# First query-weight load split over unequal DMA engines, with probability copies and key transposes regrouped on VectorE

## The chip, the cores and the metric

The kernel runs on one core of one Trainium2 chip. The metric is the device time of one execution in microseconds (us); the number given for a kernel is the median of several executions. A profile is one further execution, recorded by the hardware profiler; it gives the time from the first to the last instruction (the span), each engine's instructions, and the packets of the core's 16 DMA engines.

## The reference

One decode step for two rows of `x` (B = 2, one token each, D = 512), everything in float32. The layer-normed row `xn` feeds two branches, and both are added to `x`:

```python
q = (xn @ wq)                               # 32 heads of 128
k, v = the last W = 4096 positions of the caches, 8 kv heads, each shared by 4 q heads
p = softmax(q k^T * 128**-0.5);  o = p v
A = o @ wo                                   # (2, 4096) @ (4096, 512)
h = relu(xn @ W_gate) * (xn @ W_up)          # 1792 wide
B = h @ W_down
out = x + A + B
```

The keys and values that are needed are 2 x 8 x 4096 x 128 floats each, 32 MB and 32 MB (of 4,096 KB tiles: eight and eight); wq and wo are 8 MB each, the three GLU weights 3.5 MB each.

## The kernel before

All large inputs come in as tiles of [128 partitions x up to 32 KB] through one pool of four buffers (`ring`, line 60), and every one of these loads is issued by SyncE (`load`, lines 69 to 72, and lines 438 to 442). SyncE issues in the order of the program and waits, before each load, until the tile that used that buffer four loads earlier has been read for the last time. A load that is issued joins a queue behind the loads before it. The order is wq0, wq1, W_gate, W_up, two key tiles, then key and value tiles in turn, the last two value tiles, W_down, wo0 and wo1; wo1 goes in five pieces of 8, 4, 2, 1 and 1 rows of 2 KB per partition (line 438).

`load_wq` (lines 75 to 77) brings one half of wq: partition p holds two whole rows of wq, 32 KB that lie side by side in memory, so the load is 128 rows of 32 KB.

The work is cut in four groups g (two batches by two halves of the kv heads), each with two key tiles and two value tiles (a = 0, 1). `manual_schedule` means that each engine runs its instructions in the order in which the program writes them.

`keys(g, a, ...)` (line 243) treats a key tile in two halves mh. For each half VectorE turns 32 x 32 blocks of the key tile into `kT` (line 252). One half is 64 positions j of 64 numbers, [128 x 4096], and it is turned by CUT = 4 instructions of 16 positions each, [128 x 1024]. Then eight matmuls (line 259, order m, h, s1) add to the scores in `ss[g]`; a matmul with s1 = 0 reads the first 32 positions of `kT`, one with s1 = 1 the other 32. `kT` has two buffers.

`softmax(g)` (line 268) takes the maximum on VectorE and TensorE and writes the exponentials into `pz` on ScalarE (line 291). `turn(g)` (line 295) turns `pz` into `pT` with one VectorE instruction (line 297) and then moves 16 blocks of [32 x 256] from `pT` to `pts[g]` (line 304), the stationary operand of the value matmuls: the even ones on ScalarE, the odd ones on VectorE. `values(g, a, v)` (line 317) multiplies them by a value tile. In the loop (line 385) the keys and the softmax of group g stand ahead of the values of group g - 1, and `turn(g)` behind them; `join` and `close` (mask, gather, normalise) are put between the halves of the next key tile.

The end: the last value tiles, then `project_wide` and `project` (lines 418 to 428) with W_down, wo0 and wo1 as these land, the last piece of wo1 with four matmuls on line 426, one copy from PSUM (line 453), and two small stores (line 456).

Of the kernel before, what the change touches and what calls it, by code (L numbers as in the profile page):

```python
# [9 lines left out]
F32 = mybir.dt.float32  # L10
# [10 lines left out]
def kernel(  # L21
# [12 lines left out]
    nc = tc.nc  # L34
    P = 128
    B, _, D = x.shape
    _, HKV, SK, DH = k_cache.shape
    HQ = wq.shape[1] // DH
# [15 lines left out]
    J = W // PK  # L54
# [5 lines left out]
    ring = ctx.enter_context(tc.tile_pool(name="ring", bufs=RING))  # L60
# [8 lines left out]
    def load(name, src, shape):  # L69
        t = ring.tile(shape, F32, name=name, tag="ring")  # L70
        nc.sync.dma_start(t, src)
        return t


    def load_wq(m):
        src = wq[m * 2 * P:(m + 1) * 2 * P, :].rearrange("(p k) f -> p k f", p=P)
        return load(f"wq{m}", src, [P, 2, HQ * DH])

    def load_ff(w, name):
        return load(name, w.rearrange("(p k) f -> p k f", p=P), [P, KC, F])  # L80
# [23 lines left out]
    x2 = const.tile([B, D], F32, name="x2")  # L104
    nc.scalar.dma_start(x2, x[:, 0, :])
    wqt = [load_wq(m) for m in range(2)]

    ident = const.tile([P, P], F32, name="ident")
# [68 lines left out]
    for kc in range(KC):  # L177
        m, k = divmod(kc, 2)
# [12 lines left out]
    for kc in range(KC):  # L191
        for r in range(R):
            for c in range(C):
                n = r * C + c
# [6 lines left out]
    for r in range(R):  # L201
# [7 lines left out]
        for m in range(NB):  # L209
            src = qt[32 * m:32 * m + 32, :, :, 0].rearrange("p i (t h) b -> p b t h i", h=2)  # L210
            for x in range(Q):
                d = qz[32 * x:32 * x + 32, r * B:r * B + B, m]
                dst = bass.AP(
                    tensor=d.tensor, offset=d.offset + x * TK,
                    ap=[d.ap[0], d.ap[1], [64 + REP, NP], [32, 2], [1, REP]],
                )
# [21 lines left out]

    ss, pts = {}, {}
    osb = {}  # L240
    CUT = 4

    def keys(g, a, kt_in, steps=((), ())):

        if a == 0:
            ss[g] = ps_s.tile([P, 512], F32, name=f"s{g}", tag="s")
        for mh in range(2):
            kt = ktp.tile([P, J, 2, 32], F32, name=f"kT{g}_{a}_{mh}", tag="kT")
            src = kt_in.rearrange("p (j d) -> p j d", d=DH)[:, :, PK * mh:PK * mh + PK]
            n = J // CUT  # L250
            for c in range(CUT):
                nc.vector.transpose(  # L252
                    kt[:, c * n:(c + 1) * n].rearrange("p j m i -> p j (m i)"), src[:, c * n:(c + 1) * n]
                )
            for m in range(2):
                for h in range(2):
                    for s1 in range(S1):
                        q = 2 * h + s1
                        nc.tensor.matmul(  # L259
                            ss[g][32 * q:32 * q + 32, :], qz[:, g, 2 * mh + m, a, h], kt[:, JS * s1:JS * s1 + JS, m, h::2],  # L260
                            start=(a == 0 and mh == 0 and m == 0), stop=(a == NP - 1 and mh == 1 and m == 1),
                        )
            for step in steps[mh]:
                step()
# [30 lines left out]
    def turn(g):  # L295
        pT = work.tile([P, JS, Q, NP, REP], F32, name=f"pT{g}", tag="pT", bufs=1)
        nc.vector.transpose(pT.rearrange("p j x t k -> p (j x t k)"), pz.rearrange("p j s -> p (j s)"))  # L297
        pts[g] = work.tile([P, NP, S1, JS, 2, REP], F32, name=f"pt{g}", tag="pt")
        n = 0
        for h in range(2):  # L300
            for s1 in range(S1):
                q = 32 * (2 * h + s1)
                for x in range(Q):
                    (nc.vector.tensor_copy if n % 2 else nc.scalar.copy)(  # L304
                        pts[g][32 * x:32 * x + 32, :, s1, :, h], pT[q:q + 32, :, x].rearrange("p j t k -> p t j k")
                    )
                    n += 1

    lps = {}

# [58 lines left out]
    for a in range(NP):  # L369
        keys(0, a, load_kv(k_cache, "k", 0, a))  # L370
    softmax(0)
    turn(0)
    def join(g, a):
        mask(g, a)
# [10 lines left out]
    for g in range(1, NG):  # L385
        for a in range(NP):
            kt_in = load_kv(k_cache, "k", g, a)
            v_in = load_kv(v_cache, "v", g - 1, a)
            keys(g, a, kt_in, steps)
            if a:  # L390
                softmax(g)
            values(g - 1, a, v_in)
            if a:
                turn(g)
            steps = (
                (lambda g=g, a=a: join(g - 1, a),), (lambda g=g: close(g - 1),) if a else (),
            )
# [87 lines left out]
```

## Time and profile before

| | |
|---|---|
| median of three executions | 230.36 us (230.18 to 230.57) |
| the profiled execution, time / span | 230.8 us / 228.4 us |
| granted TensorE clock, mean over the span | 0.821 |
| TensorE matmuls busy | 143.5 us, 63% of the span |
| VectorE busy | 112.4 us, 49%, 176 instructions |
| ScalarE busy | 27.0 us, 12%, 72 instructions |
| read from HBM | 94.90 MB, 416 GB/s over the span |

How to read the profile: times in a timeline or a chain run from the first instruction. A group's row gives line, engine, operation, tiles (out<-in), shape and count, then busy time in all and the mean duration of one in ns, then the engine's idle time just before these instructions and what ended it. The row "DMA" of the page gives, for 40 equal slices of the span, how busy the 16 DMA engines were in tenths (9 is 90% or more); "GB/s" is what they moved. In a table of windows the last two columns are the mean share of the 16 DMA engines and GB/s. "SPq" is SyncE's sequencer, which issues loads. "q1", "q8", "q10" and "q14" are rows of DMA queues: q1 carries what SyncE issues, q10 what ScalarE issues, q8 and q14 carry instructions that an engine's sequencer fetches.

### The profile page before, as it was taken

What the parts mean: (1) busy time and instruction counts of PE and PEld (TensorE: products, weight loads), DVE (VectorE), ACT (ScalarE), POOL (GpSimd) and SP (SyncE); (2) the same over time, 40 slices, a digit from 0 to 9 for tenths busy, and PEclk for the clock granted to TensorE, in tenths of its full rate; (3) what the DMA queues carried; (4) which work ended last, traced back from release to release, by engine and by line L of the source; (5) the groups of instructions that cost most, each with busy time, mean ns of one, the idle gap of its engine ahead of it and who ended that gap; (6) DMA issues with size and microseconds to landing.
All of it is one profiled execution on the core that took longest, in us unless ns stands there. A gap on an engine that the chain in (4) does not pass through costs nothing.

```text
span 228.4 us, 2114 instructions
## 1 busy us (share of the span) xinstructions
PE 143.5 (63%) x864; PEld 40.1 (18%) x864; DVE 112.4 (49%) x176; ACT 27.0 (12%) x72; POOL 3.7 (2%) x11
## 2 busy tenths in 40 slices
PE   0582927806674038957499196859928757868393
PEld 0530211201111001402013011101401201214011
DVE  2300043049894499865992594797069272120000
ACT  2000123000000720003500000700000160000001
POOL 6000000000000000000000000000000000000000
PEclk9999767795999557997759859767995995999589
DMA  7999999999999999999999999999999999999991
GB/s 276 459 413 412 472 402 422 448 453 419 413 455 442 396 448 445 407 430 453 425 410 453 436 407 442 429 430 425 448 430 419 439 430 418 440 419 448 399 387 44
DMA packets 3917, 95.04 MB, mean 416 GB/s; under 512 B 442, under 2 KB 450, under 8 KB 836
## 3 DMA queue, kind: packets, MB, share of 16 engines
q1 hardware_dynamic: 3896, 94.90, 97.0%
q8 instruction: 7, 0.11, 0.2%
q14 instruction: 2, 0.02, 0.0%
q10 hardware_dynamic: 12, 0.01, 0.0%
HBM read 94.90 MB, written 0.00 MB: 416 GB/s over the span
## 4 chain that ended last, share of the span: by engine, by line
DMA 60%; DVE 21%; PE 13%; ACT 2%; issue 1%; SPq 1%; DVEq 0%; ACTq 0%
DMA k<-in_A_k_cache_dram 39%; DVE kT L252 16%; DMA wo<-in_A_wo_dram 11%; DMA wq<-in_A_wq_dram 9%; PE s L259 5%; PE o L324 4%; PE q_ps L195 2%; DVE pt L304 2%; ACT pz L291 1%; DVE pT L297 1%; DVE on L333 1%; PE oa L344 1%; SPq L441 1%; DVE m L271 1%; ACT L291 1%
## 5 line engine op out<-in xcount | busy, mean ns | idle before, releaser
L259 PE MATMUL s<-kT,qz 128*32 128x512 f32 x256 | 61.5, 780 | 43.7 <-DVE kT L252 43.7
L252 DVE STREAM_TRANSPOSE kT<-k 128x1024 f32<-128x1024 f32 x64 | 73.5, 1210 | 19.9 <-DMA k<-in_A_k_cache_dram 19.8
L324 PE MATMUL o<-v,pt 128*32 128x512 f32 x256 | 36.6, 677 | 0.0
L259 PEld LDWEIGHTS s<-kT,qz 128*32 128x32 f32 x256 | 10.7, 127 | 88.3 <-DVE kT L252 47.5
L344 PE MATMUL oa<-on,pick 128*16 128x512 f32 x16 | 12.5, 876 | 4.5 <-DVE on L333 4.5
L291 ACT ACTIVATE pz<-s,nm 64x512 f32<-64x512 f32 x8 | 5.8, 726 | 74.6 <-DVE nm L285 74.5
L195 PE MATMUL q_ps<-wq,xnT 128*32 128x512 f32 x64 | 10.9, 846 | 4.9 <-DMA wq<-in_A_wq_dram 4.9
L324 PEld LDWEIGHTS o<-v,pt 128*32 128x32 f32 x256 | 10.5, 122 | 19.9 <-issue 19.7
L304 ACT COPY pt<-pT 32x256 f32<-32x256 f32 x32 | 12.8, 401 | 5.6 <-DVE pT L297 5.2
L217 DVE COPY qz<-qt 32x32 f32<-32x32 f32 x16 | 3.0, 188 | 21.1 <-ACT qz L217 21.1
L422 PE MATMUL yw_ps<-wo,oT 128*2 128x512 f32 x56 | 8.1, 730 | 4.4 <-DMA wo<-in_A_wo_dram 4.4
L333 DVE TENSOR_TENSOR on<-o,own_u 128x512 f32<-128x512 f32 x8 | 5.4, 673 | 10.8 <-PE o L324 10.8
L453 DVE COPY yo<-y_ps 128x128 f32<-128x128 f32 x1 | 0.3, 292 | 20.2 <-PE y_ps L426 20.2
L304 DVE COPY pt<-pT 32x256 f32<-32x256 f32 x32 | 9.1, 285 | 0.5
L297 DVE STREAM_TRANSPOSE pT<-pz 128x1024 f32<-128x1024 f32 x4 | 5.0, 1246 | 8.3 <-ACT pz L291 8.3
L183 PE MATMUL xt_ps<-rep,xc 2*128 2x32 f32 x16 | 3.7, 402 | 8.4 <-DVE rep L176 8.4
L271 DVE TENSOR_REDUCE m<-s 128x1 f32<-128x512 f32 x4 | 2.8, 692 | 8.5 <-PE s L259 8.5
L225 PE MATMUL u_ps<-wu,xnT 128*32 128x448 f32 x32 | 4.8, 764 | 2.2 <-DMA wu<-in_B_W_up_dram 2.2
L291 ACT ACT_TABLE_LOAD x1 | 1.3, 1283 | 34.6 <-DVE nm L285 34.6
L183 PEld LDWEIGHTS xt_ps<-rep,xc 2*128 2x128 f32 x16 | 3.6, 319 | 8.4 <-DVE rep L176 8.4
L225 PE MATMUL g_ps<-wg,xnT 128*32 128x448 f32 x32 | 5.0, 783 | 0.0
L195 PEld LDWEIGHTS q_ps<-wq,xnT 128*32 128x32 f32 x64 | 2.7, 147 | 12.1 <-issue 6.2
(69 smaller groups left out, 56.5 us busy)
## 6 DMA issues: line engine op xcount, KB each, us to landing
k<-in_A_k_cache_dram SPq DMA_DIRECT2D x8, 4096.0 KB, 29.5
v<-in_A_v_cache_dram SPq DMA_DIRECT2D x8, 4096.0 KB, 29.2
wq<-in_A_wq_dram SPq DMA_DIRECT2D x2, 4096.0 KB, 16.7
wo<-in_A_wo_dram SPq DMA_DIRECT2D x1, 4096.0 KB, 29.7
wg<-in_B_W_gate_dram SPq DMA_DIRECT2D x1, 3584.0 KB, 29.4
wu<-in_B_W_up_dram SPq DMA_DIRECT2D x1, 3584.0 KB
wd<-in_B_W_down_dram SPq DMA_DIRECT2D x1, 3584.0 KB
wo<-in_A_wo_dram SPq DMA_DIRECT2D x1, 2048.0 KB, 22.9
```

The costliest lines, as they stand in the source:

```text
L183: nc.tensor.matmul(xt_ps[:, v, kc, :], lhsT, rep16.rearrange("r s b -> r (s b)"), start=True, stop=True)
L195: nc.tensor.matmul(q_ps[r][32 * c:32 * c + 32, :], xnT[:, 0, kc, :], wqt[kc // 2][:, kc % 2, n * 512:(n + 1) * 512], start=(kc == 0), stop ...
L225: nc.tensor.matmul(dst[32 * c:32 * c + 32, :], xnT[:, 1, kc, :], wt[:, kc, c * FQ:(c + 1) * FQ], start=(kc == 0), stop=(kc == KC - 1),)
L252: nc.vector.transpose(kt[:, c * n:(c + 1) * n].rearrange("p j m i -> p j (m i)"), src[:, c * n:(c + 1) * n])
L259: nc.tensor.matmul(ss[g][32 * q:32 * q + 32, :], qz[:, g, 2 * mh + m, a, h], kt[:, JS * s1:JS * s1 + JS, m, h::2], start=(a == 0 and mh == ...
L291: nc.scalar.activation(pv[o, :, :, h], ss[g][o].rearrange("p (j i) -> p j i", j=JS), AF.Exp, bias=nm[o], scale=SCALE, accum_out=l[o],)
L297: nc.vector.transpose(pT.rearrange("p j x t k -> p (j x t k)"), pz.rearrange("p j s -> p (j s)"))
L304: (nc.vector.tensor_copy if n % 2 else nc.scalar.copy)(pts[g][32 * x:32 * x + 32, :, s1, :, h], pT[q:q + 32, :, x].rearrange("p j t k -> p ...
L324: nc.tensor.matmul(o[32 * q:32 * q + 32, :], pts[g][:, a, s1, j:j + 4].rearrange("p u h k -> p (u h k)"), v[:, lo:lo + 512], start=(s1 == ...
L333: nc.vector.tensor_tensor(ons[a], o.rearrange("p (u d) -> p u d", u=4), own_u[:, :, None].to_broadcast([P, 4, P]), op=ALU.mult)
L344: nc.tensor.matmul(oa[g].rearrange("h u d -> h (u d)"), pick[:, 8 - 8 * a:24 - 8 * a], ons[a].rearrange("p u d -> p (u d)"), start=(a == 0 ...
L422: nc.tensor.matmul(yw_ps[32 * c:32 * c + B, :], lhsT, w, start=(n < Q), stop=(n >= wide - Q))
```

## The change

Three edits.

1. `load_wq(0)` is no longer one load of 128 rows of 32 KB. It is a load of the first 112 rows of 32 KB, a load of the first 24 KB of the last 16 rows, and four loads of the last 8 KB of four rows each (partitions 112 to 115, 116 to 119, 120 to 123, 124 to 127): six loads in place of one, on the same queue. The constants are LOW = 4 rows and OVER = 2048 numbers. The description of the change says that these 8 KB go to the four lowest load engines. `load_wq(1)` stays one load.
2. In `keys`, CUT is gone: one instruction turns each half tile, [128 x 4096].
3. In `turn`, all 16 copies are VectorE's; ScalarE makes none.

```diff
+    LOW = 4
+    OVER = 2048
+
     def load_wq(m):
-        src = wq[m * 2 * P:(m + 1) * 2 * P, :].rearrange("(p k) f -> p k f", p=P)
-        return load(f"wq{m}", src, [P, 2, HQ * DH])
+        src = wq[m * 2 * P:(m + 1) * 2 * P, :].rearrange("(p k) f -> p (k f)", p=P)
+        t = ring.tile([P, 2, HQ * DH], F32, name=f"wq{m}", tag="ring")
+        if m:
+            nc.sync.dma_start(t.rearrange("p k f -> p (k f)"), src)
+            return t
+        dst = t.rearrange("p k f -> p (k f)")
+        n = 2 * HQ * DH - OVER
+        nc.sync.dma_start(dst[0:P - 16], src[0:P - 16])
+        nc.sync.dma_start(dst[P - 16:P, 0:n], src[P - 16:P, 0:n])
+        for p in range(P - 16, P, LOW):
+            nc.sync.dma_start(dst[p:p + LOW, n:], src[p:p + LOW, n:])
+        return t
...
-    CUT = 4
...
-            n = J // CUT
-            for c in range(CUT):
-                nc.vector.transpose(
-                    kt[:, c * n:(c + 1) * n].rearrange("p j m i -> p j (m i)"), src[:, c * n:(c + 1) * n]
-                )
+            nc.vector.transpose(kt.rearrange("p j m i -> p j (m i)"), src)
...
-        n = 0
         for h in range(2):
             for s1 in range(S1):
                 q = 32 * (2 * h + s1)
                 for x in range(Q):
-                    (nc.vector.tensor_copy if n % 2 else nc.scalar.copy)(
+                    nc.vector.tensor_copy(
                         pts[g][32 * x:32 * x + 32, :, s1, :, h], pT[q:q + 32, :, x].rearrange("p j t k -> p t j k")
                     )
-                    n += 1
```

## The prediction

> **What bounds the kernel now.** I read the page first, then the chain of waits in order of time, then the loads' times from issue to landing, and last the share of the DMA engines in narrow windows at the end.
>
> ```profile
> span 228.4 us, 2114 instructions
> ...
> PE 143.5 (63%) x864; PEld 40.1 (18%) x864; DVE 112.4 (49%) x176; ACT 27.0 (12%) x72; POOL 3.7 (2%) x11
> ...
> DMA  7999999999999999999999999999999999999991
> ...
> q1 hardware_dynamic: 3896, 94.90, 97.0%
> q8 instruction: 7, 0.11, 0.2%
> q14 instruction: 2, 0.02, 0.0%
> q10 hardware_dynamic: 12, 0.01, 0.0%
> ```
>
> No compute engine is busy for more than 63%, while the 16 DMA engines are at nine tenths or more in every slice but the first and the last. The packets of q1, SyncE's loads, take 97.0% of 16 engines' span. So one engine moves 94.90 MB / (0.970 x 16 x 228.4 us) = 26.8 KB per us: 32 KB (32,768 bytes) take it 1.22 us, 24 KB 0.92 us, 8 KB 0.306 us. All 16 move 428 KB per us, so a 4,096 KB tile takes 9.8 us.
>
> The chain seems to speak for VectorE in the middle:
>
> ```profile
> 80.39 0.29 DVE pt L304
> 80.68 0.01 issue
> 80.69 9.14 DVE kT L252 x8
> ...
> 100.70 27.69 DMA k<-in_A_k_cache_dram
> ...
> 198.46 26.13 DMA wo<-in_A_wo_dram
> ```
>
> A key load that is issued at 100.70 lands 27.69 us later, but its own transfer is 9.8 us: the other 18 us it stands in the queue. VectorE decided when it was issued, not when it landed. How near this comes to mattering is in the loads' shortest time from issue to landing, first for k, then for wo:
>
> ```profile
> DMA to landing us min/median/max: 19.1/29.5/32.4
> DMA to landing us min/median/max: 22.9/26.0/29.7
> ```
>
> The worst k load still had 19.1 - 9.8 = 9.3 us of other transfers ahead of it. Delay on VectorE, TensorE or ScalarE below that costs nothing. What sets the time is the last DMA engine's share of the stream, and then the short tail:
>
> ```profile
> core 0: us, PE busy (x) PEld busy (x) DVE busy (x) ACT busy (x) POOL busy (x), PEclk, DMA share, GB/s
> 222.00:222.50 0.50, 0.40 (x4) 0.11 (x8) 0.00 (x0) 0.00 (x0) 0.00 (x0) 1.00 0.86 332
> 222.50:222.75 0.25, 0.25 (x8) 0.00 (x0) 0.00 (x0) 0.00 (x0) 0.00 (x0) 1.00 0.53 205
> 222.75:223.00 0.25, 0.25 (x4) 0.00 (x0) 0.00 (x0) 0.00 (x0) 0.00 (x0) 1.00 0.49 188
> 223.00:223.50 0.50, 0.28 (x12) 0.14 (x12) 0.00 (x0) 0.29 (x1) 0.00 (x0) 1.00 0.45 172
> 223.50:224.00 0.50, 0.50 (x24) 0.29 (x16) 0.00 (x0) 0.30 (x1) 0.00 (x0) 1.00 0.38 147
> 224.00:224.25 0.25, 0.25 (x16) 0.15 (x8) 0.00 (x0) 0.00 (x0) 0.00 (x0) 1.00 0.14 49
> ```
>
> and in the timeline behind it:
>
> ```profile
> 224.64 0.40 PE L426 MATMUL y_ps<-wo,oT 128*2 128x128 f32 x8 [0.17 <-DMA wo<-in_A_wo_dram]
> 225.11 0.29 DVE L453 COPY yo<-y_ps 128x128 f32<-128x128 f32 x1 [20.24 <-PE y_ps L426]
> 225.43 0.65 SPq L456 DMA_DIRECT2D out_dram<-yo  x1
> ```
>
> The engines do not stop together, though every one was given the same bytes. At 222.50 the share is 0.53: eight of 16 have ended. The 0.14 that is missing before that is 1.12 engine-us, so those eight ended at about 222.36. From 223.5 a share of 0.38 is six engines, and 0.14 of 16 x 0.25 us shared by six puts their end at about 224.09. So six are late by 1.73 us, two lie between, eight are early. The last piece lands at 198.46 + 26.13 = 224.59, and matmuls, copy and store follow. The cause that the page offers is q8 and q14: nine packets, some 16 KB each on q8, which single engines move besides their loads. What was left after 222.50 (0.25 x 205 + 0.25 x 188 + 0.5 x 172 + 0.5 x 147 + 0.25 x 49 = 270 KB) would take all 16 engines 0.63 us, to 223.13: no sharing out of the loads can gain more than 0.96 us.
>
> **The change, part by part.**
>
> *wq0.* Each engine had eight rows of 32 KB. It now has seven, one of 24 KB, and on four engines four more of 8 KB. Twelve engines are relieved of 8 KB, -0.306 us; four take 24 KB more, +0.918 us. No engine waits for another, the queue never runs dry before the end, so each keeps its shift to the end. If the four are early ones, they end at 222.36 + 0.92 = 223.28 and the six late ones at 224.09 - 0.31 = 223.78: the end moves by -0.31 us. New descriptors: one more row and completion on all engines, four more on the four. The nearest row is q10: 12 packets under 0.05% of 16 engines' span, so at most 0.15 us each; most q1 packets are rows that run back to back, so I take 0.02 us, and 0 to 0.3 for the range. Sum -0.29 us.
>
> [...] No view here names engines. [...]
>
> Five more issues stand on SyncE ahead of wq1:
>
> ```profile
> 0.73 0.86 SPq L71 DMA_DIRECT2D wq<-in_A_wq_dram  x2
> ...
> 12.95 5.59 PE L195 MATMUL q_ps<-wq,xnT 128*32 128x512 f32 x32 [0.88 <-DMA wq<-in_A_wq_dram]
> ...
> 22.55 5.34 PE L195 MATMUL q_ps<-wq,xnT 128*32 128x512 f32 x32 [4.01 <-DMA wq<-in_A_wq_dram]
> ```
>
> At 0.43 us each that is 2.2 us for wq1, W_gate and W_up, hidden by seven rows, 8.6 us of work, on each engine; bare it would cost 2.2 us. wq0 is whole up to 0.9 us later: the first projection then ends at 19.4 instead of 18.5, before wq1 is there at 22.5. Cost nothing.
>
> *Key transposes.*
>
> ```profile
> L252 DVE STREAM_TRANSPOSE kT<-k 128x1024 f32<-128x1024 f32 x64 | 73.5, 1210 | 19.9 <-DMA k<-in_A_k_cache_dram 19.8
> L304 ACT COPY pt<-pT 32x256 f32<-32x256 f32 x32 | 12.8, 401 | 5.6 <-DVE pT L297 5.2
> L304 DVE COPY pt<-pT 32x256 f32<-32x256 f32 x32 | 9.1, 285 | 0.5
> L118 DVE MEMSET ones<- 1x1 f32 x1 | 0.1, 59 | 0.8 <-PEq L471 0.8
> ```
>
> The last row that this part needs is of the timeline, a matmul that starts on half of a half tile:
>
> ```profile
> 62.90 1.05 PE L259 MATMUL s<-kT,qz 128*32 128x512 f32 x2 [1.01 <-DVE kT L252]
> ```
>
> 64 instructions become 16. Eight took 9.14 us, 1.14 us apart, so a half tile takes 4.57 us now. No row has 128 x 4096. If a VectorE instruction has a fixed part like the smallest row's 59 ns, three of them go, 4.39 us; if the pieces overlapped and the long one shows the whole 4 x 1.21, 4.84 us. I take 4.5, near the first. The matmuls with s1 = 0 could start after half of a half tile; in the row at 62.90 one did (two records), 1.05 us. Now it waits for all of it: at most 1.05 us later for the scores, and behind it on TensorE the rest of the half's eight and the value matmuls.
>
> *Probabilities.* ScalarE loses 8 copies of 0.401 us in each group, VectorE gains 8 of 0.30 (80.39 to 80.69): +2.4 us per group. Behind them on VectorE stand the next key tile's transposes, whose end frees a buffer that SyncE waits for. Together at most 2.4 + 1.05 + 0.5 = 4 us at the tightest place, against 9.3 us of queue, and against 22.9 - 4.9 = 18 us at wo1's first piece (2,048 KB at 428 KB per us). Both edits cost and bring nothing. Without that cover they would cost about 2 us a group, 8 us.
>
> The profiled execution would go from 230.8 to 230.5 us; it stood 0.4 us above the median, so the median goes from 230.36 to 230.07 us.
>
> **The rivals.**
>
> *Shared doors (slower).* All 16 short rows go to 16 neighbouring partitions, and the four of each small load to four adjoining ones. The mechanism: neighbouring partitions share one way into SBUF that passes no more than one engine's rate. Then the 24 KB rows, four to a way, take 3.67 us instead of 0.92 and each small load 1.22 instead of 0.31. The four engines spend 3.67 + 4.90 = 8.57 us where a 32 KB row took 1.22: +7.35, less their lead of 1.73, gives +5.6 us, 236.0. With twice the rate per way: 1.84 + 2.45 - 1.22 - 1.73 = +1.3 us, 231.7. It decides once a way passes less than some three engines' rate. For it: nothing here loads fewer than 128 partitions but the 4 KB of x, so nothing contradicts it. Against it: nothing shows it either. Chance 0.17.
>
> [...]
>
> *A late engine is among the four (slower).* Its end goes from 224.09 to 225.01: +0.92 us, 231.28. It decides as soon as one of six is hit. No view names the late engines. If fetches went to engines at random, the four would hardly ever be free; if they go round engine by engine, the late ones are neighbours. TensorE's 2 x 864 instructions draw seven packets of 16 KB, one in some 250, so its first instructions were fetched ahead of the span, and if that began at the lowest engines, these have had their turn; that is an argument and no measurement. Chance 0.10.
>
> *Nothing gained (same).* One of the two half-late engines is among the four, or the small rows are spread: 224.59 within 0.2 us, 230.3. Chance 0.15.
>
> *VectorE takes over (slower).* More than 9.3 us late at one key load, for instance if the long transposes make it wait for `kT`: some +1 us, 231.4. Chance 0.03.
>
> **How the numbers follow.** The forecast, -0.29 us, has 0.55. About 0.2% (0.46 us) is what a measurement of this kernel can tell from no change, and -0.29 us is 0.13%: most of it falls within. The three executions lie 0.39 us apart, and a fetch can fall away with the 32 ScalarE and 16 net VectorE instructions that go; so of the 0.55 I put 0.18 beyond 0.46 us faster, and 0.02 of the 0.15. Faster 0.20; same 0.37 + 0.13 = 0.50; slower 0.17 + 0.10 + 0.03 = 0.30. Low end: 230.36 - 0.66 = 229.7, the forecast with the spread. High end: 231.4, past the late engine and VectorE; shared doors are left out. The forecast's own range is 229.7 to 230.5.
>
> **What would show it.** Right: the share in the windows before the end falls later and more steeply, wo's last piece lands about 0.3 us earlier, kT has 16 instructions of 4.4 to 4.8 us, VectorE is up by 5 to 12 us, ScalarE down by 13, and k's shortest issue to landing stays above 13 us. Wrong: the wq0 loads take several us longer and the share stays near a quarter at the end (doors); a last landing about 0.6 to 0.9 us later with one engine running on (late engine); slices within the span below nine tenths (VectorE).

## The result, and the profile after

The changed kernel takes 240.84 us (240.39 to 241.16, five executions) where the kernel before takes 230.36: slower by 10.48 us, ratio 1.0445 with a 95% interval of 1.0428 to 1.0463. (A ratio is estimated from all executions, so it is not exactly the quotient of the two medians; here and below, losses are differences of medians unless "by the ratio" stands with them.) The profiled execution has a span of 238.4 us, 10.0 more than before. Its page, as the one shown of before:

```profile
span 238.4 us, 2071 instructions
...
PE 130.6 (55%) x864; PEld 38.0 (16%) x864; DVE 118.8 (50%) x160; ACT 14.2 (6%) x40; POOL 3.7 (2%) x11
...
DMA  9998999999999999999999999999999999999991
GB/s 237 264 201 190 429 430 423 436 430 440 440 429 434 434 419 418 429 432 434 434 437 440 423 440 429 423 415 434 434 434 434 440 432 423 416 447 421 418 382 39
...
q1 hardware_dynamic: 3944, 94.90, 97.0%
q8 instruction: 7, 0.11, 0.2%
...
q14 instruction: 1, 0.01, 0.0%
```

The compute rows are what was expected: VectorE is up by 6.4 us, ScalarE down by 12.8, one instruction fetch of q14 has gone. The row "DMA" shows no hole: the 16 engines are as busy as before, 97.0% on q1. The row "GB/s" has the loss: in the first four slices, some 24 us, the engines are busy and move 190 to 264 GB/s, and from the fifth slice on about 430 as before. A busy DMA engine is not an engine at full rate; the two rows have to be read against each other. The same in windows (the last two columns are the share of the DMA engines and GB/s; a packet counts whole in the window in which it starts, so a share can come out above 1), first before, then after:

```profile
4.00:12.00 8.00, 3.63 (x16) 3.56 (x16) 3.55 (x14) 0.29 (x1) 0.32 (x3) 1.00 0.92 397
12.00:20.00 8.00, 5.66 (x33) 1.43 (x32) 0.42 (x1) 0.00 (x0) 0.00 (x0) 1.00 1.05 455
20.00:28.00 8.00, 5.45 (x34) 1.47 (x35) 0.00 (x0) 0.59 (x1) 0.00 (x0) 0.79 0.95 410
28.00:36.00 8.00, 3.64 (x20) 1.55 (x23) 3.06 (x14) 2.29 (x13) 0.00 (x0) 0.66 1.06 459
60.00:200.00 140.00, 93.88 (x540) 23.81 (x533) 91.35 (x126) 20.72 (x50) 0.00 (x0) 0.80 1.00 430
```

```profile
4.00:12.00 8.00, 3.63 (x16) 3.56 (x16) 3.54 (x14) 0.29 (x1) 0.31 (x3) 1.00 0.96 254
12.00:20.00 8.00, 0.06 (x1) 0.00 (x0) 0.42 (x1) 0.00 (x0) 0.00 (x0) 1.00 1.07 187
20.00:28.00 8.00, 6.24 (x32) 1.57 (x32) 0.00 (x0) 0.00 (x0) 0.00 (x0) 1.00 0.89 333
28.00:36.00 8.00, 2.46 (x12) 0.59 (x16) 0.00 (x0) 0.00 (x0) 0.00 (x0) 0.65 0.98 421
60.00:200.00 140.00, 77.62 (x490) 20.36 (x490) 104.32 (x112) 7.90 (x18) 0.00 (x0) 0.77 1.00 431
```

From 4 to 28 us the kernel before moves 8 x (397 + 455 + 410) = 10,096 KB, the changed one 8 x (254 + 187 + 333) = 6,192 KB. The 3,904 KB that are missing are 9.1 us at 428 KB per us. From 28 to 36 us another 8 x (459 - 421) = 304 KB are missing, 0.7 us. In the long middle the rates are 430 and 431. So 9.8 of the 10.0 us are lost in the first 36 us, nearly all of it while wq0 comes in, and nothing is lost or won in the middle.

One more row of after, from SyncE's own waits, looks like a cause and is none:

```profile
SPq L71 <- DMA wq<-in_A_wq_dram: 24.5, 5, 14.2
```

SyncE held the load of W_up back for 14.2 us, until the first piece of wq0 had landed (before, it was issued at 2.11 us). But the DMA engines had other loads queued all that time, or the row "DMA" would show a hole.

### The profile page after: what moved, and what is told of

Read it like the earlier page. It is cut to its first block, busy times and chain, and to the rows that moved or that the text cites. A ratio compares the mean times of both kernels' runs of the same rounds, so it can differ in the third digit from the quotient of the medians.

```text
span 238.4 us, 2071 instructions
## 1 busy us (share of the span) xinstructions
PE 130.6 (55%) x864; PEld 38.0 (16%) x864; DVE 118.8 (50%) x160; ACT 14.2 (6%) x40; POOL 3.7 (2%) x11
## 4 chain that ended last, share of the span: by engine, by line
DMA 59%; DVE 20%; PE 13%; issue 3%; ACT 2%; SPq 2%; DVEq 0%; ACTq 0%
DMA k<-in_A_k_cache_dram 36%; DVE kT L262 13%; DMA wq<-in_A_wq_dram 13%; DMA wo<-in_A_wo_dram 10%; PE s L267 4%; DVE pt L311 4%; PE o L330 4%; PE q_ps L208 2%; PE oa L350 1%; ACT pz L299 1%; DVE pT L305 1%; DVE on L339 1%; SPq L447 1%; SPq L89 1%; DVE m L279 1%
## 5 line engine op out<-in xcount | busy, mean ns | idle before, releaser
L262 DVE STREAM_TRANSPOSE kT<-k 128x4096 f32<-128x4096 f32 x16 | 70.6, 4429 | 13.6 <-DMA k<-in_A_k_cache_dram 13.5
L267 PE MATMUL s<-kT,qz 128*32 128x512 f32 x256 | 44.8, 824 | 57.3 <-DVE kT L262 57.3
L330 PE MATMUL o<-v,pt 128*32 128x512 f32 x256 | 33.5, 656 | 0.0
L267 PEld LDWEIGHTS s<-kT,qz 128*32 128x32 f32 x256 | 9.2, 132 | 86.8 <-issue 62.3
L311 DVE COPY pt<-pT 32x256 f32<-32x256 f32 x64 | 18.2, 285 | 1.0
L350 PE MATMUL oa<-on,pick 128*16 128x512 f32 x16 | 11.7, 825 | 6.9 <-DVE on L339 6.9
L330 PEld LDWEIGHTS o<-v,pt 128*32 128x32 f32 x256 | 8.7, 118 | 19.5 <-issue 19.4
L459 DVE COPY yo<-y_ps 128x128 f32<-128x128 f32 x1 | 0.3, 291 | 17.3 <-PE y_ps L432 17.3
L219 PE MATMUL qt<-ident,qs 128*128 128x128 f32 x8 | 1.6, 345 | 4.4 <-DVE qs L216 4.4
L368 PEld LDWEIGHTS op<-osb,spread 16*128 16x128 f32 x32 | 3.7, 186 | 1.8 <-DVE osb L363 0.9
L350 PEld LDWEIGHTS oa<-on,pick 128*16 128x16 f32 x16 | 1.6, 115 | 15.0 <-DVE on L339 9.6
```

What stands on the lines that cost most here:

```text
L262: nc.vector.transpose(kt.rearrange("p j m i -> p j (m i)"), src)
L267: nc.tensor.matmul(ss[g][32 * q:32 * q + 32, :], qz[:, g, 2 * mh + m, a, h], kt[:, JS * s1:JS * s1 + JS, m, h::2], start=(a == 0 and mh == ...
L311: nc.vector.tensor_copy(pts[g][32 * x:32 * x + 32, :, s1, :, h], pT[q:q + 32, :, x].rearrange("p j t k -> p t j k"))
L330: nc.tensor.matmul(o[32 * q:32 * q + 32, :], pts[g][:, a, s1, j:j + 4].rearrange("p u h k -> p (u h k)"), v[:, lo:lo + 512], start=(s1 == ...
L350: nc.tensor.matmul(oa[g].rearrange("h u d -> h (u d)"), pick[:, 8 - 8 * a:24 - 8 * a], ons[a].rearrange("p u d -> p (u d)"), start=(a == 0 ...
```

## The experiments

Theories: **A**, rows that are written at the same time to partitions that share a way into SBUF hold each other up (the rival "shared doors"); **B**, the number of loads, their short rows or SyncE's waits; **C**, VectorE has become the bound; later **D**, the places in memory that are read together. All edits are to the kernel before, in `load_wq(0)` unless said otherwise, and only added lines are shown; `dst` and `src` are wq0 as [128 x 8192] in SBUF and in memory.

### Which of the three edits

`e1_compute_only` has the change's `keys` and `turn` and the old `load_wq`; `e2_load_only` the new `load_wq` and the old rest.

> The two VectorE edits alone (one transpose per half tile, all 16 copies of a group on VectorE), with wq0 as one load of 128 rows. Theory A (shared ways into SBUF: rows that are written at the same time into neighbouring partitions hold each other up): the whole +10.5 us comes from the wq0 loads, so this stands at 230.4 us within 0.5. Theory B (many loads: six loads in place of one, with short rows, late issues and waits of SyncE): the same 230.4. Theory C (VectorE became the bound): 238 to 241 us.

> The six wq0 loads alone, with the transposes in four pieces and the copies shared by ScalarE and VectorE as before. Theory A and theory B: 240 to 241 us, all of the loss. Theory C: 230.4 us.

Measured: e1 230.48 us, ratio 0.9998 (0.9989 to 1.0008); e2 240.65 us, ratio 1.0446 (1.0418 to 1.0475). The load is the whole loss; theory C has fallen. The VectorE edits cost and bring nothing, and e1's profile says why. Its groups, and the last line of what it says of k:

```profile
L249 DVE STREAM_TRANSPOSE kT<-k 128x4096 f32<-128x4096 f32 x16 | 70.6, 4429 | 15.7 <-DMA k<-in_A_k_cache_dram 15.6
L298 DVE COPY pt<-pT 32x256 f32<-32x256 f32 x64 | 18.2, 285 | 1.0
...
DMA to landing us min/median/max: 17.3/29.7/32.2
```

A long transpose takes 4.43 us. The shortest k load still lands 17.3 us after its issue, 19.1 before the edits: the delay of 1.8 us is there, and 17.3 - 9.8 = 7.5 us of queue are still ahead of that load.

### The shape of the pieces

```diff
+        # e3_112_16
+        nc.sync.dma_start(dst[0:P - 16], src[0:P - 16])
+        nc.sync.dma_start(dst[P - 16:P], src[P - 16:P])
+        # e4_six_wide
+        cuts = (0, 4096, 6144, 6656, 7168, 7680, 8192)
+        for c0, c1 in zip(cuts, cuts[1:]):
+            nc.sync.dma_start(dst[:, c0:c1], src[:, c0:c1])
```

> The kernel before, with wq0 as two loads, the first 112 rows and the last 16 rows, all rows whole (32 KB): no short row, no four-row load, and SyncE has one more load to issue. Theory A: 112 rows and 16 rows spread over the engines in another way than 128 rows do, so several engines write neighbouring partitions at once; most of the loss stays, 236 to 240 us. Theory B: 230.4 to 231 us.

> The kernel before, with wq0 as six loads that are all 128 partitions wide: 16 KB, 8 KB and four times 2 KB of every row. As many loads on SyncE as in the change, and shorter rows. Theory A: each load covers all partitions, 230.4 us within 0.5. Theory B: the loss is here again, 236 to 241 us.

Measured: e3 239.71 us, ratio 1.04 (1.0378 to 1.0421); e4 231.02 us, ratio 1.002 (1.0002 to 1.0037). Two whole-row loads lose 9.2 us; six loads of the full width, with rows down to 2 KB, lose about half a microsecond. Theory B has fallen but for that half. Where e3 loses, in the same windows:

```profile
4.00:12.00 8.00, 3.62 (x16) 3.57 (x16) 3.55 (x14) 0.29 (x1) 0.32 (x3) 1.00 0.98 258
12.00:20.00 8.00, 0.08 (x1) 0.00 (x0) 0.42 (x1) 0.00 (x0) 0.00 (x0) 1.00 1.12 201
20.00:28.00 8.00, 4.97 (x32) 1.31 (x32) 0.00 (x0) 0.00 (x0) 0.00 (x0) 1.00 0.81 332
```

These are nearly the changed kernel's rates, without a short row and without a four-row load. Both pieces are slow. The times from issue to landing of wq's loads, first before (wq0, then wq1 as the longest), then in e3 (the 112 rows, the 16 rows, wq1):

```profile
DMA to landing us min/median/max: 12.1/16.7/21.3
```

```profile
DMA to landing us min/median/max: 18.5/21.7/30.8
```

The 112 rows land 18.5 us after their issue, 6.4 us later than all 128 did before; the 16 rows behind them bring the rest.

### Which rows are in flight together

```diff
+        # e5_halves
+        for h in range(2):
+            nc.sync.dma_start(dst[64 * h:64 * h + 64], src[64 * h:64 * h + 64])
+        # e6_even_odd
+        for h in range(2):
+            nc.sync.dma_start(dst[h:P:2], src[h:P:2])
```

> The kernel before, with wq0 as two loads of 64 rows of 32 KB, partitions 0 to 63 and then 64 to 127. Theory B (number and shape of loads) is left with nothing: 230.4 to 231 us, as for six wide loads. Theory A asks how many of the 16 engines write neighbouring partitions at once. If engines take neighbouring rows in turn, 16 neighbouring partitions are written at once as in the 112 rows: 238 to 241 us. If each engine takes its own run of four neighbouring rows, two engines at most share a way: 230.4 us if a way passes twice one engine's rate, 236 to 240 us if it passes one.

> The same two loads of 64 rows of 32 KB, but the even partitions first and then the odd ones: same engines, bytes, rows and number of loads as the two halves, other partitions at the same time. Theory A with neighbouring rows in turn: 16 rows over 32 partitions at once, half as many engines to a way as with the halves, so clearly less than the halves cost, 231 to 236 us. Theory A with a run of rows for each engine: the same as the halves. Theory B: the same as the halves.

Measured: e5 240.91 us, ratio 1.0455 (1.0437 to 1.0472); e6 230.81 us, ratio 1.0013 (1.0004 to 1.0023). The two differ in nothing but which 64 of the 128 rows come together, and by 10.1 us. First e5, then e6:

```profile
4.00:12.00 8.00, 3.63 (x16) 3.56 (x16) 3.55 (x14) 0.29 (x1) 0.31 (x3) 1.00 1.00 205
12.00:20.00 8.00, 0.07 (x1) 0.00 (x0) 0.42 (x1) 0.00 (x0) 0.00 (x0) 1.00 1.12 233
```

```profile
4.00:12.00 8.00, 3.63 (x16) 3.56 (x16) 3.55 (x14) 0.29 (x1) 0.31 (x3) 1.00 1.06 459
12.00:20.00 8.00, 5.04 (x33) 1.33 (x32) 0.42 (x1) 0.00 (x0) 0.00 (x0) 1.00 1.03 446
```

Neighbouring rows come at half the rate, 205 and 233 GB/s, at a full share of the DMA engines; even and odd rows at the whole rate. For e6 theory A had two guesses of how rows are dealt to the engines: with neighbouring rows taken in turn 231 to 236 us, with a run of neighbouring rows for each engine the same loss as e5. Both missed, so these runs do not tell how the rows are dealt.

Extra loads measure the same for the small pieces of the change. wq0 is one load here, and four loads of four rows of 16 KB, issued between wq0 and wq1, go to a spare buffer (the second buffer of `kT`, unused so early) that nothing reads.

```diff
+        nc.sync.dma_start(dst, src)
+        spare = ktp.tile([P, 4096], F32, name="spare", tag="kT")
+        for i in range(4):
+            rows = slice(112 + 4 * i, 116 + 4 * i)     # e7_extra_near
+            rows = slice(112 + i, 128, 4)              # e8_extra_apart
+            nc.sync.dma_start(spare[rows], src[rows, 4096:8192])
```

> The kernel before with wq0 as one load, and four more loads of four rows of 16 KB into a spare buffer that nothing reads: 256 KB of extra reading. Here the four rows of each load lie in neighbouring partitions (112 to 115 and so on), as the small loads of the change. On four engines that is 64 KB more each, 2.45 us at 26.8 KB per us. Theory A: four rows share one way; 4.9 us if it passes twice one engine's rate, 9.8 us if once; less the lead of 1.73 us of early engines: +3.2 to +8 us, 233.5 to 238.5. Theory B: as with rows apart, about 231 to 233 us.

> The same four extra loads of four rows of 16 KB, but each load takes partitions 112, 116, 120, 124 (then 113 and so on): same engines, bytes and rows, no two neighbours in one load. Theory A: no way is shared by the four, 2.45 us on four engines; if these are early ones (lead 1.73 us, the assumption of the prediction) +0.7 us, 231.1 us; if a late one is among them +2.4 us, 232.8. Theory B: the same as with neighbouring rows.

Measured: e7 239.4 us, ratio 1.0386 (1.0361 to 1.0411); e8 234.6 us, ratio 1.0187 (1.0161 to 1.0212). Neighbours cost 4.8 us more than rows four apart, as theory A has it. But e7 lost 9.0 us, more than the 3.2 to 8 that were expected, and e8 lost 4.2 us where theory A, as it stood, expected 0.7 or 2.4: partitions 112, 116, 120 and 124 are not free either.

### SBUF or memory

In all runs so far row and partition go together, so the places in memory could be the cause as well. e9 and e10 cross the two (x is put in the same order by one small VectorE copy); e11 and e12 do the same with the extra loads.

```diff
+        # e9_to_halves
+        for h in range(2):
+            nc.sync.dma_start(dst[64 * h:64 * h + 64], src[h:P:2])
+        # e10_from_halves
+        for h in range(2):
+            nc.sync.dma_start(dst[h:P:2], src[64 * h:64 * h + 64])
+        # e11_near_from_apart
+            nc.sync.dma_start(spare[112 + 4 * i:116 + 4 * i], src[112 + i:128:4, 4096:8192])
+        # e12_apart_from_near
+            nc.sync.dma_start(spare[112 + i:128:4], src[112 + 4 * i:116 + 4 * i, 4096:8192])
```

> The kernel before, with wq0 as two loads of 64 rows: the even rows of memory go to partitions 0 to 63, the odd ones to partitions 64 to 127 (x is put in the same order by one small VectorE copy, so the result is the reference's). Rows and partitions were tied together so far; here memory is read as in the even/odd load (230.8 us) and SBUF is written as in the halves (240.9 us). Theory A, shared ways into SBUF: 240 to 242 us. Theory D, the loss comes from the places in memory that are read at the same time: 230.5 to 231.5 us.

> The other way round: memory rows 0 to 63 go to the even partitions, then rows 64 to 127 to the odd ones. Memory is read as in the halves, SBUF is written as in the even/odd load. Theory A: 230.5 to 231.5 us. Theory D: 240 to 242 us.

> The four extra loads of four rows of 16 KB into the spare buffer, to neighbouring partitions (112 to 115 and so on), but from memory rows that lie four rows apart. Theory A: as with neighbours on both sides, 238.5 to 240 us. Theory D: as with rows apart on both sides, 234 to 235 us.

> The same four extra loads to partitions four apart (112, 116, 120, 124 and so on), from neighbouring memory rows. Theory A: 234 to 235 us. Theory D: 238.5 to 240 us.

Measured: e9 241.03 us, ratio 1.0459 (1.0444 to 1.0475); e10 231.12 us, ratio 1.003 (1.0018 to 1.0041); e11 239.11 us, ratio 1.0377 (1.0349 to 1.0405); e12 235.03 us, ratio 1.0197 (1.018 to 1.0214). All four follow the partitions and not the memory; theory D has fallen. First e9, then e10:

```profile
4.00:12.00 8.00, 3.31 (x16) 3.31 (x16) 3.83 (x15) 0.29 (x1) 0.32 (x3) 1.00 1.07 221
```

```profile
4.00:12.00 8.00, 3.32 (x16) 3.32 (x16) 3.83 (x15) 0.29 (x1) 0.31 (x3) 1.00 1.04 451
```

### Which partitions share a way, and whether the four engines are early

A guess that fitted the half rate of 64 neighbours is **map 2** in the expectations: eight neighbouring partitions share one way, so that 128 have 16 ways, 64 neighbours 8, 32 have 4 and 16 have 2, and the rate would halve at each step. e13 and e16 try that; e14 and e15 put the extra loads of e8 at partitions 0, 4, 8, 12 and at 16, 20, 24, 28 (then at the next of each, as in e8).

```diff
+        # e13_quarters: n = 32; e16_eighths: n = 16
+        for h in range(0, P, n):
+            nc.sync.dma_start(dst[h:h + n], src[h:h + n])
+            # e14_extra_own, e15_extra_other: the extra loads of e8, at other partitions
+            rows = slice(i, 16, 4)                     # e14_extra_own
+            rows = slice(16 + i, 32, 4)                # e15_extra_other
```

> The kernel before, with wq0 as four loads of 32 neighbouring rows of 32 KB. [...] With map 2 (eight neighbours to a way) 32 neighbours reach 4 ways: a quarter of the rate for 4,096 KB, 3 x 9.8 = 29 us more, 258 to 262 us.

> The kernel before, with wq0 as eight loads of 16 neighbouring rows of 32 KB. [...] With map 2 they reach 2 ways, an eighth: 69 us more, about 300 us. [...]

> The kernel before with wq0 as one load, and four extra loads of four rows of 16 KB into the spare buffer, at partitions 0, 4, 8, 12 (then 1, 5, 9, 13 and so on). [...] With map 2 two of the four share a way: 234 to 235.5 us, as at 112, 116, 120, 124.

> [...] With map 2 also 234 to 235.5 us, the same as the run at partitions 0, 4, 8, 12.

Measured: e13 240.44 us, ratio 1.0425 (1.0398 to 1.0452); e16 256.75 us, ratio 1.1145 (1.1097 to 1.1192); e14 232.35 us, ratio 1.0066 (1.0043 to 1.0089); e15 234.59 us, ratio 1.0174 (1.014 to 1.0209). First e13, then e16:

```profile
4.00:12.00 8.00, 3.63 (x16) 3.56 (x16) 3.54 (x14) 0.29 (x1) 0.31 (x3) 1.00 1.00 205
12.00:20.00 8.00, 0.06 (x1) 0.00 (x0) 0.42 (x1) 0.00 (x0) 0.00 (x0) 1.00 1.15 238
```

```profile
4.00:12.00 8.00, 3.63 (x16) 3.56 (x16) 3.55 (x14) 0.29 (x1) 0.31 (x3) 1.00 1.15 131
12.00:20.00 8.00, 0.07 (x1) 0.00 (x0) 0.42 (x1) 0.00 (x0) 0.00 (x0) 1.00 1.15 131
20.00:28.00 8.00, 0.00 (x0) 0.00 (x0) 0.00 (x0) 0.00 (x0) 0.00 (x0) 1.00 0.65 74
28.00:36.00 8.00, 0.00 (x0) 0.00 (x0) 0.00 (x0) 0.00 (x0) 0.00 (x0) 1.00 1.08 123
```

32 neighbours come at the same rate as 64 (205 and 238 against 205 and 233), 16 at about half of that, (131 + 131 + 74 + 123) / 4 = 115 GB/s. Map 2 would have halved the rate from 64 to 32; it has fallen, and e16 ended far below its 300 us. What stands is the measured rates, from 4 us on: about 430 GB/s for 128 partitions, 219 in pieces of 64 neighbours, 222 in pieces of 32, 115 in pieces of 16. The second 32 of 64 neighbours added nothing to the rate of the first, while 32 came at twice the rate of 16. Which partitions share a way is not shown beyond that.

The extra loads depend on their place too. At partitions 0, 4, 8, 12 (e14) they cost 1.5 us by the ratio, where map 2 expected as much as at 112, 116, 120, 124; at 16, 20, 24, 28 (e15) they cost some 4.0, as at 112, 116, 120, 124 (e8). In e14 they slow nobody: 513 and 360 GB/s in its two windows below, against 328 and 197 in e15. Why partitions 0 to 15 are better off is not shown. First e14, then e15:

```profile
12.00:15.00 3.00, 1.99 (x13) 0.69 (x16) 0.42 (x1) 0.00 (x0) 0.00 (x0) 1.00 1.20 513
15.00:18.00 3.00, 3.00 (x27) 0.64 (x16) 0.00 (x0) 0.00 (x0) 0.00 (x0) 1.00 0.83 360
```

```profile
12.00:15.00 3.00, 1.75 (x9) 0.46 (x12) 0.42 (x1) 0.00 (x0) 0.00 (x0) 1.00 1.39 328
15.00:18.00 3.00, 3.00 (x20) 0.90 (x16) 0.00 (x0) 0.00 (x0) 0.00 (x0) 1.00 0.66 197
```

e14 is also the clean measurement of who is early: four engines carry 64 KB more each, 2.45 us, and hinder nobody. Its windows at the end:

```profile
222.50:223.00 0.50, 0.50 (x8) 0.10 (x4) 0.00 (x0) 0.00 (x0) 0.00 (x0) 1.00 0.67 266
...
223.50:224.00 0.50, 0.50 (x12) 0.07 (x8) 0.00 (x0) 0.00 (x0) 0.00 (x0) 1.00 0.61 238
224.00:224.50 0.50, 0.50 (x12) 0.06 (x8) 0.00 (x0) 0.00 (x0) 0.00 (x0) 1.00 0.26 102
224.50:225.00 0.50, 0.50 (x8) 0.00 (x0) 0.00 (x0) 0.00 (x0) 0.00 (x0) 1.00 0.23 90
225.00:225.50 0.50, 0.32 (x12) 0.31 (x16) 0.00 (x0) 0.42 (x1) 0.00 (x0) 1.00 0.15 57
225.50:226.00 0.50, 0.50 (x24) 0.28 (x17) 0.00 (x0) 0.16 (x1) 0.00 (x0) 1.00 0.08 29
```

Ten engines until 224.0 (0.61 of 16), then four (0.26), and these four do not stop together: about 2.4 engines on average from 225.0, 1.3 from 225.5. With 2.45 us more, an early engine of before (222.36) should end at about 224.8; two do so within some 0.4 us, two run about 0.8 us longer. In the kernel before two engines lay between the early and the late ones, and in e14 the only place left for them is among these four: ten engines are left at 224.0, six late ones and the four.

## Why the prediction was wrong

**What bounds the kernel: right.** Loads decide; the two compute edits alone measured 0.9998, and a load that is slow at the start is paid in full at the end (9.8 us missing at 36 us, 10.0 at the end of the span).

**wq0: the step that failed** is "No engine waits for another, the queue never runs dry before the end, so each keeps its shift to the end". Where the rows of a load go to neighbouring partitions only, the engines hold each other up: pieces of 64 neighbours came at 219 GB/s (e5), of 32 at 222 (e13) and of 16 at 115 (e16), as much as 8.2, 8.3 and 4.3 engines move at 26.8 KB per us (26.8 GB/s), while even and odd rows came at 459 and 446 GB/s (e6). In e7 engines without an extra row were held up too (last section). The share of the DMA engines does not show it: it stays at 1.0 with half the bytes. The term that was taken as -0.306 us (12 engines) and +0.918 us (four) measured +10.2 us alone (e2); the whole change lost 10.5. That the small loads use four engines fits the pages, by an estimate: packets under 512 bytes are 442 before, of which 27 loads by 16 engines would be 432, and 474 after, and the 32 more would be 16 for the load of 16 rows and four for each small load. That these four are the lowest engines, no run shows.

**The rival "shared doors" is what happened**, with a chance of 0.17, and it was mis-sized: 1.3 to 5.6 us for the small loads and the 24 KB rows alone. Most of the loss came from the piece that was taken for harmless, the 112 rows and the 16 behind them: 9.2 us with whole rows (e3). Why these are slow is not shown: how the 112 rows are dealt to the engines was not measured, and e6 does not fit a run of neighbours for each engine. The condition given for the rival (a way passes less than three engines' rate) fits e16, where 16 neighbours came at 115 GB/s, 29 for each four of them, near one engine's 26.8 GB/s. The rival also laid the cost on the four engines, so that they would run on at the end with a share near a quarter. In the changed kernel no four engines run on; the share falls to nothing within some 2 us, as before the change:

```profile
232.00:233.00 1.00, 0.90 (x8) 0.11 (x8) 0.00 (x0) 0.00 (x0) 0.00 (x0) 1.00 0.66 254
233.00:234.00 1.00, 0.79 (x28) 0.43 (x25) 0.00 (x0) 0.58 (x1) 0.00 (x0) 1.00 0.23 86
234.00:234.50 0.50, 0.47 (x16) 0.17 (x8) 0.00 (x0) 0.00 (x0) 0.00 (x0) 1.00 0.01 4
```

So the loss fell on all engines alike.

**The four early engines: half right.** By e14 two of the four are early and two are the half-late ones, if four-row loads at other partitions use the same four engines, which no run shows. The fetches fit this in number: within the stream of the kernel before lie six packets of q8 and, smaller, two of q14, and six engines are late and two lie between; that the fetches are the cause was not tried. A half-late engine with 0.92 us more would end at about 225.8 - 2.45 + 0.92 = 224.3, near the 224.09 of the late ones. So by this estimate the change would have gained nothing even without sharing, as the rival "Nothing gained" has it, if one of the four is half-late in the changed kernel too, which has one fetch of q14 left.

**The bare price of five more issues: right that it is hidden.** Six wide loads cost 0.5 us (e4), even and odd rows 0.3 us (e6), both by the ratio, small beside the 2.2 us of issue time. That SyncE would then wait 14.2 us for wq0's first piece to land was not foreseen; the queue covered it.

**Key transposes and probabilities: right.** A long transpose took 4.43 us (4.5 taken), VectorE rose by 6.4 us and ScalarE fell by 12.8, k's shortest time to landing fell by 1.8 us (at most 4 expected), and the time did not move.

**No faster version came out of this.** e14 shows that four engines can carry 64 KB more each without slowing the others (513 and 360 GB/s from 12 to 18 us), but no run lifted work from the late engines, so whether that would gain anything is not shown.

## What to carry to other kernels

When all DMA engines are busy, look at bytes per microsecond beside the busy share: contention shows in the first alone. Cut a large load along its rows' length and leave it 128 partitions wide; pieces made of fewer neighbouring partitions came slower (219 GB/s in pieces of 64, 222 of 32, 115 of 16, against about 430; 112 rows landed 6.4 us later than 128), and here the load at the head of the queue passed its loss to the end of the kernel undiminished. Before moving bytes to "idle" engines, ask where the bytes land (the same extra loads cost 1.5 us at partitions 0 to 15 and 4.0 at 16 to 31), and measure which engines are idle with extra loads that hinder nobody.

## What the runs showed that was not expected

- More engines are held up than those with an extra row. In e15 suppose that the four engines with extra rows hold up four others, for about 5 us (sixteen rows of 16 KB at half rate, four to an engine: 4 x 1.22). If only those eight went at half rate, 8 x 0.5 x 4.9 x 26.8 = 525 KB would be missing between 12 and 18 us; against e14 3 x (513 + 360 - 328 - 197) = 1,044 KB are, about twice as much, what all 16 engines at half rate would miss. In e7, where the four rows of each extra load are neighbours, the twelve engines without an extra row would alone move 12 x 26.8 = 322 KB per us if they were not held up; 175 GB/s were moved from 12 to 15 us and 153 from 15 to 18. Why the others slow down too stays open.
- 64 rows at every second partition, two loads one after the other, come at the full rate (459 and 446 GB/s in e6). 128 partitions in one load were not needed here; 64 neighbours came at half that rate (205 and 233 GB/s in e5).
